# Seven small moves ahead of the first attention slot: first exponential, maxima, clearings, and who subtracts

## The chip, the cores and the metric

The kernel runs on one core of one Trainium2 chip. The metric is device time in microseconds (us); lower is better. A core has a matrix engine (TensorE, PE in the profile, its weight loads PEld), VectorE (DVE), ScalarE (ACT), GpSimd (POOL) and SyncE (SP), which here issues every DMA. Each engine works through its own instructions in order and waits at semaphores for the others. SBUF is the memory that all engines read and write; TensorE's results land in eight banks of PSUM.

## What is computed

`x` is 2048 x 512. With `xn` the row-normalised `x`, the output is attention times a gate, added to `x`:

```python
def _A_ref(x, wqkv, wo):                       # H = 32 heads of Dh = 16, window W = 256
    qkv = (x @ wqkv).reshape(B, S, 3, H, Dh).transpose(2, 0, 3, 1, 4)
    scores = jnp.einsum("bhqd,bhkd->bhqk", q, k) * (Dh ** -0.5)
    mask = (idx[:, None] - idx[None, :] >= 0) & (idx[:, None] - idx[None, :] < W)
    p = softmax(jnp.where(mask, scores, -1e9))
    return einsum(p, v).reshape(B, S, D) @ wo

def _B_ref(x, w1, b1, w2, b2):                 # F = 1792
    y = _layernorm(x)
    return _gelu(y @ w1 + b1) @ w2 + b2

return x + _A_ref(xn, ...) * _silu(_B_ref(xn, ...))
```

## The kernel before

**High and low parts.** Every matmul operand is split into a rounded high part and the rest, the low part, and a product is made of three passes (high x high, high x low, low x high; `PASSES`, line 67). The high part is a cast on ScalarE, the low part a subtraction on VectorE or GpSimd.

**Slots.** Attention is written as slots `t` = -16 to 128 (loop at line 896), one block of 128 queries of a group of four heads per slot: `prob_block` makes transposed scores in the PSUM tile `stb`, exponentiates them on ScalarE into `pt` and masks them on GpSimd (`affine_select`); it is called twice a slot, for head pair 1 and then for pair 0. `pv_step` multiplies with the values `vt` one slot later. `max_block(m)`, with m = t + 12, makes the plain scores in `xy` and `zo`, and VectorE masks them (`copy_predicated`) and reduces them to row maxima `mt`. `max_rows` sends the maxima of four blocks through DRAM (`mT_d`) into a row of the tile `slots[i]` (called qk0 and qk1), which holds the queries and keys of a head group.

**Projections fill the slots.** What TensorE does beside this in a slot is cut into two halves, `fill_in(t, 0)` and `fill_in(t, 1)`; `fills` says which matmuls stand in which half, `plan` what other work stands in a slot, `ends` (through `behind`) what ends it. Everything is emitted in that order, which is the order of every engine's queue, SP's too. `later(k, f)` puts f off by k halves. Slots -16 to -1 have no `prob_block`; in slots -8 to -1 the maxima block stands between the two halves.

**Jobs by halves.** `job_qk(n, c)` projects queries and keys of head group n for 512 tokens, `job_v(0, i)` the values of 256 tokens. From slot -8 on, `by_halves` runs such a job in two phases of 12 units; a unit is two matmuls side by side on the upper and lower 64 rows of the array, each into a bank of its own, and the second phase exchanges the banks. Before the second phase starts, the first must be through. That is seen to by a wait on a marker: for jobs with `by_max` it is the masked copy of the last maxima block, for the others a small memset of a column of the tile `sv` on GpSimd, which itself waits for the last unit. Jobs alternate between the banks `fb` (two tiles) and two banks of the pool `ps_st` (`others`, named pair_-8_599 and so on in the trace). At slot 0 that pool is closed, and `stb` takes its place.

**After a job.** For values, ScalarE copies the banks to `vt`. For queries and keys of group 1 (n = 1), ScalarE copies the banks to `pjr` (`raw`), casts it to `sh` (`hi`), and GpSimd subtracts. For group 0, ScalarE casts straight from the two banks and VectorE subtracts straight from them (lines 323 to 336). SP then issues four DMAs of the high part and two of the low part into `slots`.

**Other work.** `clear_part(k)` writes zeros or ones to a quarter of `slots[1]` on ScalarE, in slots -4 to -1 (lines 898 to 901). Slot 1's place in SBUF is that of the tile `x23`, which holds x for chunks 2 and 3; `job_x(3)` in slot -6 transposes the last of it, through `fb` and `ps_st`, into `xnT`. `split_wqk` makes the high part `wqb` of the weights of group 1 in slot -5 and the low part at the end of slot -4.

Of the kernel before, what the change touches and what calls it, by code (L numbers as in the profile page):

```python
# [9 lines left out]
F32 = mybir.dt.float32  # L10
# [5 lines left out]
PSUM = bass.MemoryType.PSUM  # L16

S, D, H, DH, WIN, F = 2048, 512, 32, 16, 256, 1792
P = 128
# [31 lines left out]
def mixer_kernel(ctx, tc, x, wqk, wv, wo, w1, b1, w2, b2, out):  # L51
# [132 lines left out]
    stb = []  # L184
# [96 lines left out]
    def later(k, fn):  # L281

        if k == 0:
            fn()
        else:
            h = 2 * now[0] + now[1] + k
            delayed.setdefault((h // 2, h % 2), []).append(fn)

    def job_qk(n, c):

        box = []
        ops = [(kt, a, b) for kt in range(KT) for a, b in PASSES]
        if not n and c < 3:
            ops.sort(key=lambda o: o[2])
        sl = slice(512 * c, 512 * (c + 1))

        def mm(i):
            if i == 0:
                box.append(fill_bank() if c else xy[:, 0])
            kt, a, b = ops[i]  # L300
            nc.tensor.matmul(box[0], wqs[n][:, a, kt], big[:, b, kt, sl],
                             start=(i == 0), stop=(i == len(ops) - 1))

        def half(bank, j, i, r, **flags):
            kt, a, b = ops[i]
            return nc.tensor.matmul(bank[:, 0:256], wqs[n][r, a, kt],
                                    big[r, b, kt, 512 * c + 256 * j: 512 * c + 256 * (j + 1)], **flags)

        def send(src, qk, tt):
            copy_rows(slots[n % 2][tt:P:4, qk, :, sl], src[64 * qk: 64 * qk + 64])  # L310

        def finish():
            hi = sgp.tile([P, 512], F32R, tag="sh", name=f"sh_{n}_{c}", bufs=2)
            raw = t2.tile([P, 512], F32, tag="t2", name=f"pjr_{n}_{c}")
            lo = raw.bitcast(F32R)
            if n:
                for j, bank in enumerate(box):
                    nc.scalar.copy(raw[:, 256 * j: 256 * (j + 1)], bank[:, 0:256])
                box[:] = [raw]
            wide = 512 // len(box)  # L320
            parts = [(bank[:, 0:wide], slice(wide * j, wide * (j + 1))) for j, bank in enumerate(box)]

            def high():
                for src, at_ in parts:
                    nc.scalar.copy(hi[:, at_], src)
                behind(now[0], send_high)

            def send_high():
                for qk, tt in ((1, 0), (0, 0), (1, 2), (0, 1)):
                    send(hi, qk, tt)  # L330

            def low():
                for src, at_ in parts:
                    (nc.gpsimd if n else nc.vector).tensor_tensor(lo[:, at_], src, hi[:, at_].bitcast(F32),
                                                                  op=ALU.subtract)
                behind(now[0], send_low)

            def send_low():
                send(lo, 1, 1)
                send(lo, 0, 2)  # L340

            later(1 if n else 0, high)
            later(3 if n else int(c < 3), low)
        if n or c > 1:
            return half, finish, box
        return [(216, mm, i) for i in range(len(ops))], finish

    def by_halves(job, banks, first, second, by_max=False):

        half, finish, box = job  # L350
        box[:] = banks
        seen = []
        for phase, where in enumerate((first, second)):
            for i in range(12):
                flags = dict(start=(phase == 0 and i == 0), stop=(phase == 1 and i == 11), skip_group_check=True)

                def unit(i=i, phase=phase, flags=flags):
                    if phase == 0 and i == 0:
                        box[:] = [bank() if callable(bank) else bank for bank in box]
                    two = (half(box[1 - phase], 1 - phase, i, slice(64, P), **flags),  # L360
                           half(box[phase], phase, i, slice(0, 64), **flags))
                    if phase == 0 and i == 11 and not by_max:
                        seen.append(nc.gpsimd.memset(sv[:, 31:32], 0.0))
                        for r in two:
                            tc.add_manual_dep(seen[0].ins, r.ins.name, ORDER, reason="the rows are through")
                    if phase == 1 and i == 0:
                        for r in two:
                            tc.add_manual_dep(r.ins, (seen or outs["max"])[0].ins.name, ORDER, reason="the banks change rows")
                fills.setdefault(where[len(where) * i // 12], []).append((unit, ()))
        fills[second[-1]].append((finish, ()))  # L370

    def job_v(hf, i):

        box = []

        def mm(k):
            if k == 0:
                box.append(ps_st.tile([P, 2, 256], F32, tag="b", name=f"pv_{hf}_{i}"))
            j, kt, (a, b) = k // 12, k % 12 // 3, PASSES[k % 3]
            kb = 2 * i + j  # L380
            nc.tensor.matmul(box[0][:, j], big[:, a, kt, P * kb: P * (kb + 1)], wva[:, b, kt],
                             start=(k % 12 == 0), stop=(k % 12 == 11))

        def half(bank, j, k, r, **flags):
            kt, (a, b) = k // 3, PASSES[k % 3]
            kb = 2 * i + j
            return nc.tensor.matmul(bank[:, 0:256], big[r, a, kt, P * kb: P * (kb + 1)], wva[r, b, kt], **flags)

        def finish():
            if i < 4:  # L390
                nc.scalar.copy(vt[:, 2 * i: 2 * i + 2, :, 0:DH], box[0].rearrange("p b (h d) -> p b h d", d=DH))
                return
            for j, bank in enumerate(box):
                nc.scalar.copy(vt[:, 2 * i + j, :, 0:DH], bank[:, 0:256].rearrange("p (h d) -> p h d", d=DH))
        if i > 3:
            return half, finish, box
        return [(109, mm, k) for k in range(24)], finish
# [336 lines left out]
    def at(t, fn, *args):  # L734
        plan.setdefault(t, []).append((fn, args))
# [61 lines left out]
        return ps_st.tile([P, 512], F32, tag="b", name=f"pair_{now[0]}")  # L797

    others = [free_bank, free_bank]
    for job, banks, first, second, *by_max in (  # L800
            (job_qk(0, 2), fb, [(-8, 0)], [(-7, 0)], True), (job_v(0, 4), others, [(-8, 0), (-8, 1)], [(-7, 1)]),
            (job_v(0, 5), fb, [(-5, 0)], [(-4, 0)], True), (job_qk(0, 3), others, [(-5, 1)], [(-4, 1)]),
            (job_v(0, 6), fb, [(-3, 0)], [(-2, 0)], True), (job_qk(1, 0), others, [(-3, 1)], [(-2, 1)]),
            (job_v(0, 7), fb, [(-1, 0)], [(-1, 1)]), (job_qk(1, 1), fb, [(0, 1), (1, 0)], [(2, 0), (2, 1)])):
        by_halves(job, banks, first, second, *by_max)
    fills.update(spread([job_x(3)], [(-6, 0), (-6, 1)]))
    fills[-10, 0][:0] = fills[-11, 1][-5:]
    del fills[-11, 1][-5:]
# [80 lines left out]
    def fill_in(t, half):  # L889
        now[:] = t, half  # L890
        run(delayed.pop((t, half), ()))
        for fn, args in fills.get((t, half), ()):
            fn(*args)

    end = 16 * NQ
    for t in range(-16, end + 1):
        m = t + LEAD
        if t == -5:
            open_slot(1)
            for k in range(4):  # L900
                at(-4 + k, clear_part, k)
        if 0 <= t < end:
            if t == 0:
                early.close()
                stb.append(attn.enter_context(tc.tile_pool(name="ps_s2", bufs=1, space=PSUM)).tile(
                    [P, 2, 512], F32, name="stb"))
            prob_block(t // 16, t % 16, 1)
        if t >= 0 and m < end:
            max_block(m // 16, m % 16, m not in IN_PLACE)
        fill_in(t, 0)  # L910
        for fn, args in plan.get(t, []):
            fn(*args)
        if 4 <= m < LEAD:
            max_block(0, m)
        if 0 <= t < end:
            prob_block(t // 16, t % 16, 0)
        fill_in(t, 1)
        if 0 <= m < 4:
            max_block(0, m)
        if t >= 0 and m + 1 < end and (m + 1) % 16 >= 2 and m + 1 not in IN_PLACE:  # L920
            first_scores((m + 1) // 16, (m + 1) % 16)
        if t >= 1:
            pv_step((t - 1) // 16, (t - 1) % 16)
        run(lns.get(t, ()))
        if 0 <= m < end and m % 4 == 3:
            max_rows(m // 16, m % 16 // 4, t)
        for fn, args in ends.get(t, []):
            fn(*args)
# [481 lines left out]
```

## Time and profile before

| | us |
|---|---|
| median of 3 runs | 737.11 (736.62 to 737.22) |
| the profiled execution | 736.99 |
| its span | 735.2 |
| TensorE busy | 720.2 |
| VectorE, ScalarE, GpSimd busy | 499.1, 426.0, 317.4 |

The attention slots that the change touches lie between 36 and 67 us of the span; slots 0 to 127 go on to about 424 us, and the MLP follows. TensorE's granted clock is full in all of the 40 slices. In a timeline row the columns are the start in us, the time until the last of the merged instructions ended, the engine, the operation, output<-inputs, the shape, the count, and in brackets the idle time in front with the engine that ended it. All instructions have the line 43, that of the helper which records them, so they are told apart by their tiles. A matmul's time is its way through the pipeline: starts, not durations, give the pace. In a row of stretches, the first number behind the stretch is its length, then come the busy times of PE, PEld, DVE, ACT and POOL with their instruction counts, the granted clock, the DMA engines' share and GB/s.

### The profile page before, as it was taken

Reading aid. Unit: us, or ns where it says so; the run is one execution under the profiler, and the core shown is the slowest. Engines: PE = TensorE matmul, PEld = TensorE weight load, DVE = VectorE, ACT = ScalarE, POOL = GpSimd, SP = SyncE. Lnnn points to the kernel's source line nnn. Section 1 sums busy time; section 2 is a strip of 40 time slices with the busy share of each in tenths; the row PEclk is TensorE's granted clock in tenths of the full one; section 3 lists DMA queues with packets and bytes.
Section 4 is the critical chain, followed back from the end, with each engine's and each line's share of the span. In section 5 each row is a group of like instructions: output and inputs, shape, how many; then the busy total and the mean of one; then the engine's idle time right before and its main releaser. Section 6 shows DMA issues by size and latency. Waiting matters only on the chain.

```text
span 735.2 us, 19063 instructions
## 1 busy us (share of the span) xinstructions
PE 720.2 (98%) x7584; PEld 586.3 (80%) x7584; DVE 499.1 (68%) x738; ACT 426.0 (58%) x721; POOL 317.4 (43%) x674
## 2 busy tenths in 40 slices
PE   8999999999999999999999999999999999999997
PEld 7988777777778887777776788888887888888886
DVE  6876767877766777777872666546687855666823
ACT  7747777868777676887877736232343734542001
POOL 7413667867677665777877640113202000001102
PEclk9999999999999999999999999999999999999999
DMA  8324256777766733667614376447223322153701
GB/s 296 78 47 105 66 146 162 216 233 213 209 187 189 205 121 103 164 170 199 194 63 160 105 256 165 180 130 242 87 57 101 115 73 86 60 185 115 247 23 58
DMA packets 61528, 106.77 MB, mean 145 GB/s; under 512 B 12096, under 2 KB 12352, under 8 KB 61440
## 3 DMA queue, kind: packets, MB, share of 16 engines
q1 hardware_dynamic: 61440, 105.56, 49.1%
q8 instruction: 60, 0.98, 0.5%
q14 instruction: 28, 0.23, 0.1%
HBM read 54.53 MB, written 33.82 MB: 120 GB/s over the span
## 4 chain that ended last, share of the span: by engine, by line
PE 90%; ACT 5%; DVE 2%; issue 1%; POOL 1%; DMA 1%; DVEq 0%; ACTq 0%; POOLq 0%
PE acc L43 20%; PE fb L43 19%; PE zo L43 13%; PE stb L43 9%; PE p L43 9%; PE s L43 6%; PE h L43 6%; PE xy L43 5%; ACT pt L43 3%; PE pv L43 1%; ACT x L43 1%; DVE xnT L43 1%; DVE xy L43 0%; ACT xnT L43 0%; DMA x<-in_x_dram 0%
## 5 line engine op out<-in xcount | busy, mean ns | idle before, releaser
L43 POOL TENSOR_SCALAR_AFFINE_SELECT pt<-pt 128x256 f32<-128x256 f32 x480 | 193.7, 428 | 99.6 <-ACT pt L43 94.4
L43 ACT ACTIVATE pt<-stb 128x768 f32<-128x768 f32 (+1 forms) x244 | 188.8, 774 | 45.4 <-PE stb L43 39.0
L43 DVE TENSOR_REDUCE mt<-xy 128x4 f32<-128x1024 f32 (+1 forms) x128 | 152.6, 1192 | 4.4
L43 DVE COPY_PREDICATED xy<-upper,zo 128x512 f32<-128x512 int32 x112 | 77.9, 695 | 73.8 <-PE xy L43 65.4
L43 POOL TENSOR_TENSOR xo<-xo,gated 128x512 f32<-128x512 f32 x15 | 20.0, 1331 | 220.9 <-DVE gated L43 219.9
L43 PE MATMUL zo<-pt,vt 128*17 128x128 f32 x2880 | 103.7, 275 | 0.0
L43 PE MATMUL stb<-qk 64*128 64x384 f32 (+1 forms) x488 | 94.9, 383 | 5.7 <-ACT pt L43 4.3
L43 PE MATMUL fb<-xnT,wqb 64*128 64x512 f32 (+2 forms) x732 | 99.6, 381 | 0.0
L43 PE MATMUL acc<-w,gh 128*128 128x512 f32 x320 | 98.6, 389 | 0.0
L43 PEld LDWEIGHTS stb<-qk 64*128 64x128 f32 x488 | 45.7, 183 | 49.2 <-ACT pt L43 40.3
L43 PEld LDWEIGHTS zo<-pt,vt 128*17 128x17 f32 x2880 | 67.5, 97 | 15.3 <-issue 4.9
L43 PEld LDWEIGHTS acc<-w,gh 128*128 128x128 f32 x320 | 60.1, 188 | 12.5
L43 PEld LDWEIGHTS fb<-xnT,wqb 64*128 64x128 f32 (+1 forms) x732 | 62.8, 185 | 6.5 <-DVE xy L43 0.2
L43 PE MATMUL acc<-w,gl 128*128 128x512 f32 x160 | 62.4, 390 | 0.2 <-DVE gl L43 0.2
L43 PE MATMUL xy<-qk 64*128 64x256 f32 (+2 forms) x536 | 58.4, 290 | 0.7 <-DVE mt L43 0.7
L43 PE MATMUL p<-xnT 128*128 128x512 f32 x189 | 51.8, 389 | 0.0
L43 PEld LDWEIGHTS xy<-qk 64*128 64x128 f32 x536 | 46.7, 185 | 6.1 <-issue 2.4
L43 ACT COPY oraw<-zo 128x128 f32<-128x128 f32 x108 | 28.8, 266 | 36.9 <-PE zo L43 30.1
L43 ACT ACTIVATE gated<-acc 128x512 f32<-128x512 f32 x16 | 8.7, 596 | 62.4 <-DVE acc L43 62.4
L43 PE MATMUL s<-wos,ohl 128*128 128x512 f32 (+1 forms) x204 | 44.3, 377 | 0.0
L43 PEld LDWEIGHTS s<-wos,ohl 128*128 128x128 f32 x204 | 36.8, 188 | 7.1
L43 PEld LDWEIGHTS p<-xnT 128*128 128x128 f32 x189 | 35.5, 188 | 7.4
(198 smaller groups left out, 1190.8 us busy)
## 6 DMA issues: line engine op xcount, KB each, us to landing
qk<-sh SPq DMA_DIRECT2D x128, 128.0 KB
qk<-pjr SPq DMA_DIRECT2D x64, 128.0 KB
oT_d<-oraw SPq DMA_DIRECT2D x32, 256.0 KB
w_d<-in_w_dram SPq DMA_DIRECT2D x14, 512.0 KB
xt_d<-xnT SPq DMA_DIRECT2D x12, 512.0 KB
x<-in_x_dram SPq DMA_DIRECT2D x16, 256.0 KB
w<-w_d SPq DMA_DIRECT2D x16, 256.0 KB
or<-oT_d SPq DMA_DIRECT2D x16, 256.0 KB
```

Of the source, the lines that this page charges most:

```text
L43: r = issue(*args, **kwargs)
```

## The change

- `job_qk(0, 3)` orders its units like the other chunks of group 0: those with the high part of xnT first.
- `job_qk(0, 2)` and `job_qk(0, 3)` now end as those of group 1 do: ScalarE copies the banks to `raw` and casts from there, GpSimd subtracts. The low part of chunk 3 comes one half later.
- The marker is named with each job: for `job_v(0, 4)` a memset on VectorE, for the other jobs that had a memset still one on GpSimd.
- `job_v(0, 7)`: its first phase spreads over both halves of slot -1, so that maxima block 11 stands after 6 units instead of 12, and its second phase is a third part of the slot.
- Between these two parts of slot -1 the pool is closed, `stb` is opened and the first `prob_block` of slot 0 (pair 1: scores, exponential, masks) is emitted, which stood at the head of slot 0.
- The four clearings stand in slots -5, -5, -4 and -3 instead of -4, -3, -2 and -1.

```diff
         ops = [(kt, a, b) for kt in range(KT) for a, b in PASSES]
-        if not n and c < 3:
+        if not n:
             ops.sort(key=lambda o: o[2])
...
-            if n:
+            if n or c > 1:
                 for j, bank in enumerate(box):
                     nc.scalar.copy(raw[:, 256 * j: 256 * (j + 1)], bank[:, 0:256])
                 box[:] = [raw]
...
-                    (nc.gpsimd if n else nc.vector).tensor_tensor(lo[:, at_], src, hi[:, at_].bitcast(F32),
+                    (nc.gpsimd if n or c > 1 else nc.vector).tensor_tensor(lo[:, at_], src, hi[:, at_].bitcast(F32),
                                                                   op=ALU.subtract)
...
-            later(3 if n else int(c < 3), low)
+            later(3 if n else 1, low)
...
-    def by_halves(job, banks, first, second, by_max=False):
+    def by_halves(job, banks, first, second, seer=None):
...
-                    if phase == 0 and i == 11 and not by_max:
-                        seen.append(nc.gpsimd.memset(sv[:, 31:32], 0.0))
+                    if phase == 0 and i == 11 and seer:
+                        seen.append(seer[0].memset(seer[1], 0.0))
...
-            (job_qk(0, 2), fb, [(-8, 0)], [(-7, 0)], True), (job_v(0, 4), others, [(-8, 0), (-8, 1)], [(-7, 1)]),
-            (job_v(0, 5), fb, [(-5, 0)], [(-4, 0)], True), (job_qk(0, 3), others, [(-5, 1)], [(-4, 1)]),
-            (job_v(0, 6), fb, [(-3, 0)], [(-2, 0)], True), (job_qk(1, 0), others, [(-3, 1)], [(-2, 1)]),
-            (job_v(0, 7), fb, [(-1, 0)], [(-1, 1)]), (job_qk(1, 1), fb, [(0, 1), (1, 0)], [(2, 0), (2, 1)])):
+    by_pool, by_dve = (nc.gpsimd, sv[:, 31:32]), (nc.vector, sv[:, 30:31])
+            (job_qk(0, 2), fb, [(-8, 0)], [(-7, 0)]), (job_v(0, 4), others, [(-8, 0), (-8, 1)], [(-7, 1)], by_dve),
+            (job_v(0, 5), fb, [(-5, 0)], [(-4, 0)]), (job_qk(0, 3), others, [(-5, 1)], [(-4, 1)], by_pool),
+            (job_v(0, 6), fb, [(-3, 0)], [(-2, 0)]), (job_qk(1, 0), others, [(-3, 1)], [(-2, 1)], by_pool),
+            (job_v(0, 7), fb, [(-1, 0), (-1, 1)], [(-1, 2)], by_pool),
+            (job_qk(1, 1), fb, [(0, 1), (1, 0)], [(2, 0), (2, 1)], by_pool)):
...
             for k in range(4):
-                at(-4 + k, clear_part, k)
-        if 0 <= t < end:
-            if t == 0:
-                early.close()
-                stb.append(...)
+                at(max(-5, k - 6), clear_part, k)
+        if 0 < t < end:
             prob_block(t // 16, t % 16, 1)
...
         fill_in(t, 1)
+        if t == -1:
+            early.close()
+            stb.append(...)
+            prob_block(0, 0, 1)
+            fill_in(t, 2)
```

More of the change, by code (lines that the diff above doesn't have):

```diff
@@ L799, in mixer_kernel @@
     others = [free_bank, free_bank]
-    for job, banks, first, second, *by_max in (
-            (job_qk(0, 2), fb, [(-8, 0)], [(-7, 0)], True), (job_v(0, 4), others, [(-8, 0), (-8, 1)], [(-7, 1)]),
-            (job_v(0, 5), fb, [(-5, 0)], [(-4, 0)], True), (job_qk(0, 3), others, [(-5, 1)], [(-4, 1)]),
-            (job_v(0, 6), fb, [(-3, 0)], [(-2, 0)], True), (job_qk(1, 0), others, [(-3, 1)], [(-2, 1)]),
-            (job_v(0, 7), fb, [(-1, 0)], [(-1, 1)]), (job_qk(1, 1), fb, [(0, 1), (1, 0)], [(2, 0), (2, 1)])):
-        by_halves(job, banks, first, second, *by_max)
+    by_pool, by_dve = (nc.gpsimd, sv[:, 31:32]), (nc.vector, sv[:, 30:31])
+    for job, banks, first, second, *seer in (
+            (job_qk(0, 2), fb, [(-8, 0)], [(-7, 0)]), (job_v(0, 4), others, [(-8, 0), (-8, 1)], [(-7, 1)], by_dve),
[3 more added lines that the diff above has]
+            (job_qk(1, 1), fb, [(0, 1), (1, 0)], [(2, 0), (2, 1)], by_pool)):
+        by_halves(job, banks, first, second, *seer)
     fills.update(spread([job_x(3)], [(-6, 0), (-6, 1)]))
@@ L900, in mixer_kernel @@
             for k in range(4):
-                at(-4 + k, clear_part, k)
-        if 0 <= t < end:
-            if t == 0:
-                early.close()
-                stb.append(attn.enter_context(tc.tile_pool(name="ps_s2", bufs=1, space=PSUM)).tile(
-                    [P, 2, 512], F32, name="stb"))
+                at(max(-5, k - 6), clear_part, k)
+        if 0 < t < end:
             prob_block(t // 16, t % 16, 1)
@@ L917, in mixer_kernel @@
         fill_in(t, 1)
+        if t == -1:
+            early.close()
+            stb.append(attn.enter_context(tc.tile_pool(name="ps_s2", bufs=1, space=PSUM)).tile(
+                [P, 2, 512], F32, name="stb"))
+            prob_block(0, 0, 1)
+            fill_in(t, 2)
         if 0 <= m < 4:
```

## The prediction

> **What bounds the kernel now.** I read the page first, then the busy times by stretch, then the waits and the timeline around every edit.
>
> ```profile
> span 735.2 us, 19063 instructions
> PE 720.2 (98%) x7584; PEld 586.3 (80%) x7584; DVE 499.1 (68%) x738; ACT 426.0 (58%) x721; POOL 317.4 (43%) x674
> ...
> 40.00:42.00 2.00, 0.94 (x16) 0.81 (x14) 1.79 (x2) 0.40 (x2) 1.14 (x3) 1.00 0.24 52
> 42.00:64.00 22.00, 21.57 (x322) 20.23 (x318) 16.04 (x25) 13.34 (x20) 0.30 (x3) 1.00 0.33 72
> 64.00:72.00 8.00, 7.14 (x96) 5.83 (x94) 6.43 (x10) 5.48 (x10) 5.05 (x12) 1.00 0.57 135
> 72.00:424.00 352.00, 346.35 (x5490) 271.53 (x5489) 248.06 (x315) 267.84 (x456) 247.86 (x580) 1.00 0.59 163
> ```
>
> TensorE is busy for 720.2 of 735.2 us, so an edit of the schedule can win only its idle time. The stretch rows (length, then TensorE's busy time) say where that lies: 1.06 us are lost between 40 and 42, 0.43 between 42 and 64, 0.86 between 64 and 72. All edits lie in slots -8 to 0, about 36 to 67 us. The stretch up to 424 us loses 5.65 us in small waits, each counted from work shortly before it and none from a fixed time, so I take a lead that stands at 72 us to last to the end. The profiled execution took 736.99 us, its span 735.2 with 1.8 around it; the median of the runs is 737.11. I work out the gain in the profiled execution and subtract it from the median, 0.12 above.
>
> **The change part by part.** *1. The memset of job_v(0,4) goes from GpSimd to VectorE.*
>
> ```profile
> 38.00 1.23 DVE L43 TENSOR_REDUCE mt<-xy 128x4 f32<-128x1024 f32 x1
> 38.02 1.70 PE L43 MATMUL fb<-xnT,wqb 64*128 64x256 f32 x24
> 39.55 0.40 PE L43 MATMUL xy<-qk 64*128 64x256 f32 x4
> 39.57 1.53 POOL L43 TENSOR_SCALAR x<-x,nm,rss 128x512 f32<-128x512 f32 x2
> 39.75 0.65 ACT L43 CAST sh<-fb 128x256 fp32r<-128x256 f32 x2 [1.10 <-PE fb L43]
> 41.04 0.10 POOL L43 MEMSET sv<- 128x1 f32 x1
> 41.19 0.38 PE L43 MATMUL pair_-8_599<-wva,xnT 64*128 64x256 f32 x1 [1.06 <-POOL sv L43]
> 42.05 0.74 DVE L43 TENSOR_TENSOR pjr<-fb,sh 128x256 fp32r<-128x256 f32 x2
> 42.82 1.09 PE L43 MATMUL fb<-ident,x 128*128 128x128 f32 x8
> ...
> 60.39 1.60 PE L43 MATMUL fb<-wva,xnT 64*128 64x256 f32 x24
> 61.83 0.40 PE L43 MATMUL xy<-qk 64*128 64x256 f32 x4
> 62.27 1.69 PE L43 MATMUL fb<-wva,xnT 64*128 64x256 f32 x24
> 62.45 0.70 DVE L43 COPY_PREDICATED xy<-upper,zo 128x512 f32<-128x512 int32 x1 [1.38 <-PE zo L43]
> 63.18 1.23 DVE L43 TENSOR_REDUCE mt<-xy 128x4 f32<-128x1024 f32 x1
> ```
>
> The second phase starts at 41.19 because the memset stands in GpSimd's queue behind two normalisations of x (39.57 to 41.10). A maxima block's matmuls take 0.44 us up to the next work (61.83 to 62.27); counted from 39.55 the phase could start at 39.99. On VectorE the memset stands behind a reduction ending at 39.23. Its cost there isn't in the trace: 0.10 as on GpSimd, or at most the 0.70 of a masked copy. Either ends by 39.93, in time; I take 0.10. Nobody waits behind it: the next masked copy waits for TensorE. Gain 1.20.
>
> What is late next? The transposes of x (42.82), which follow the phase, move to 41.62. Their x is ready at 41.10. They write fb, which VectorE's subtraction of job_qk(0,2) reads until 42.79: alone, the memset's move would win almost nothing. *2. That subtraction goes to GpSimd*, from a copy in SBUF, so fb is free after ScalarE's copies (40.40), and the whole 1.20 stands. It costs ScalarE one more 512-wide cast (0.63, from the 46.10 row below; ends near 41.0, and its next work is due at 41.7) and GpSimd 1.28 (the 66.20 row), behind the x tiles: 41.10 to 42.4, where VectorE ended at 42.79. SP's four high sends start 0.6 later, and the low ones behind them; the maxima block that reads them stands at 51.39, so even 1.20 sooner they have some 5 us.
>
> *3. Job_qk(0,3) likewise, and the clearings sooner.*
>
> ```profile
> 44.45 1.09 PE L43 MATMUL tr<-ident,x 128*128 128x128 f32 x8
> 46.10 0.63 ACT L43 CAST wqb<-wqkr 128x512 fp32r<-128x512 f32 x1
> 51.39 0.52 PE L43 MATMUL xy<-qk 64*128 64x256 f32 x4
> 51.59 0.65 ACT L43 COPY vt<-fb 128x256 f32<-128x256 f32 x2 [4.86 <-PE fb L43]
> 52.12 1.92 ACT L43 ACTIVATE qk<-vt 128x2048 fp32r<-128x2048 f32 x1
> 52.85 1.23 DVE L43 TENSOR_REDUCE mt<-xy 128x4 f32<-128x1024 f32 x1
> 53.29 1.72 PE L43 MATMUL fb<-wva,xnT 64*128 64x256 f32 x24
> 55.01 0.68 DVE L43 TENSOR_TENSOR wqb<-wqkr,wqb 128x512 fp32r<-128x512 f32 x1
> 55.43 0.28 PE L43 MATMUL pair_-3_927<-xnT,wqb 64*128 64x256 f32 x1
> 55.75 0.38 PE L43 MATMUL pair_-3_928<-xnT,wqb 64*128 64x256 f32 x1
> 57.16 1.18 SPq L43 DMA_DIRECT2D qk<-pjr  x2
> 58.69 0.65 ACT L43 COPY vt<-fb 128x256 f32<-128x256 f32 x2 [2.29 <-PE fb L43]
> 66.20 1.28 POOL L43 TENSOR_TENSOR pjr<-pjr,sh 128x512 fp32r<-128x512 f32 x1
> ```
>
> Units of a pair follow each other by 0.12 us (60.39 to 61.83 for twelve). The third unit of job_qk(1,0) should stand at 55.55 and stands at 55.75: it waits for the low part of wqb, which VectorE makes behind two subtractions of job_qk(0,3). With these gone it follows the reduction that ends at 54.08, so 52.9 to 53.6 with the lead of 1.20, against a need at 54.35. Gain 0.20.
>
> ScalarE's work is hidden by idle time. Clearings 0 and 1 follow the cast of wqb: 46.10 less 1.20 plus 0.63 is 45.53, plus 2 x 1.92 is 49.4; the next copies are due at 51.59 - 1.20 = 50.39, and ScalarE idles 4.86 before them now. Clearing 2 follows these copies to 52.9; then the copies out of job_qk(0,3)'s banks (0.65, to 53.6), whose next writer, job_qk(1,0), comes at 55.43 less two units and the lead, 54.0: 0.4 to spare. Cast (to 54.2) and clearing 3 (to 56.1) end ahead of the copies at 58.69 - 1.40 = 57.3. GpSimd's subtraction runs 54.2 to 55.5; its sends now stand in SP's queue behind a return of row maxima, so I put their issue at 58 to 59.2 instead of 57.16 to 58.34. They are read at 62.8 (below). Sorting the units changes their order, not their number: nothing.
>
> [...]
>
> *4. The boundary of slots -1 and 0.*
>
> ```profile
> 59.84 1.23 DVE L43 TENSOR_REDUCE mt<-xy 128x4 f32<-128x1024 f32 x1
> 62.12 0.10 POOL L43 MEMSET sv<- 128x1 f32 x1 [4.68 <-PE fb L43]
> 64.46 0.51 PE L43 MATMUL xy<-qk 64*128 64x256 f32 x4 [0.32 <-DVE mt L43]
> 65.44 0.44 PE L43 MATMUL stb<-qk 64*128 64x384 f32 x2 [0.30 <-ACT pt L43]
> 65.72 0.87 PE L43 MATMUL fb<-xnT,wqb 64*128 64x256 f32 x12
> 65.91 1.23 DVE L43 TENSOR_REDUCE mt<-xy 128x4 f32<-128x1024 f32 x1
> 67.19 0.50 PE L43 MATMUL xy<-qk 64*128 64x256 f32 x4
> ```
>
> I count from job_v(0,7)'s first unit (60.39 before). Now: fb of job_qk(1,1) at +5.33, the maxima block of slot 1 at +6.80. After: six units, 0.72; maxima block 11 (the reduction it waits for ends at 61.07, +0.68, just in time), 0.44; six units, the last issued at +1.76; first scores, 0.28 (65.44 to 65.72), to +2.16. The second phase waits for GpSimd's memset: before, it started 0.56 after the last unit's issue (61.71 to 62.27), so +2.32, a wait of 0.16. Twelve units to +3.76; block 12, 0.44; second scores, 0.28; so fb at +4.48. ScalarE must have copied fb: with ScalarE free, copies began 0.41 after a job's last unit (38.02 + 11 x 0.12 = 39.34, to 39.75) and took 0.65, so +3.64 + 1.06 = +4.70. TensorE would gain 0.63. VectorE: block 12's masked copy 0.62 after its matmuls (61.83 to 62.45), reduction 0.73 later, 1.23 long: +6.34, so slot 1's block at +6.39; TensorE itself would be there at +4.70 + 1.47 = +6.17. VectorE comes last: gain 0.41, bounds 0.41 and 0.63. Both waits named in the rows go; the exponential no longer ends them.
>
> Sum: 1.20 + 0.20 + 0.41 = 1.81, by the upper bound 2.03. 737.11 - 1.81 = 735.3, 0.25% less.
>
> **The rivals.** *VectorE's loop takes part 4.* Masked copy and reduction, 2 us with the matmuls between, already end only 0.04 ahead of block 11. If they or the memset cost 0.4 more, only 1.40 is left: 735.7. For it: part 4 already ends on VectorE; against: the extra must last past slot 2.
>
> *Part 1 moves its wait.* If the transposes still wait, for x, fb or ScalarE, 0.3 of the 1.20 is won: with the rest 0.9, 736.2. For it: three things must be ready at 41.6. Against: the latest is x, 0.5 ahead. [...]
>
> *Slower: the clearings stand in front.* Slot 1's place holds x until the transposes (44.45 plus 1.09, less 1.20: 44.3). Were it free late, clearings 0 and 1 would hold up ScalarE's copies of job_v(0,5), which free fb for the matmuls at 53.29. The copies have 1.0 to spare and fb another 1.0 (53.29 - 1.20 against 50.39 + 0.65), so every us of start beyond 47.6 costs TensorE one; beyond 49.4 the gain is gone. If the first started where it does now (52.12 - 1.20 = 50.9), 3.3 is lost: 738.6. Against: no row has a reader of x after the transposes.
>
> *The change does not do what it says*, the scores being held by the pool that they are moved into: then part 4 alone falls, the first rival's 735.7.
>
> **How the numbers follow.** About 0.2% (1.47 us, 735.64) is what a measurement of this kernel can tell from no change. Forecast 0.70 (735.3, own range 734.8 to 735.7, of which 0.06 lies above 735.64); part 4 lost, for either cause, 0.15 (735.7, a third of it below 735.64); moved wait or lock 0.10 (736.2 to 736.4); slower 0.05 (738.6). Faster: 0.64 + 0.05 = 0.69; same 0.25; slower 0.06 with unnamed mishaps. The range reaches down to 734.6 for small waits of 64 to 72 us that may go beyond the 2.03, and up to 736.6 for the moved wait; what it leaves out is the slower case and edges.
>
> **What would show it.** Right: no TensorE wait for sv near 40; transposes of x near 41.6; TensorE idle between 40 and 42 near 0.1; four clearings ended by 56.5; the first exponential near 61, ahead of job_v(0,7)'s copies; slot 1's maxima block near 65.4, not 67.19; the same lead at 424. Wrong: a wait for fb, x or wqb in its place, ScalarE clearing past 50, or a lead that shrinks later.

## The result, and the profile after

The changed kernel takes 735.17 us (median of 18 runs, 734.74 to 736.18) against 736.88 for the kernel before (18 runs beside them); the ratio is 0.9978, 95% interval 0.9972 to 0.9985, or 1.7 us less. The forecast was 735.3 within 734.6 to 736.6.

The page's head of the changed kernel and its stretches, columns as before:

```profile
span 734.4 us, 19062 instructions
PE 721.2 (98%) x7584; PEld 588.1 (80%) x7584; DVE 498.6 (68%) x735; ACT 427.7 (58%) x723; POOL 319.5 (44%) x675
...
40.00:42.00 2.00, 2.00 (x38) 2.00 (x36) 1.02 (x4) 1.27 (x3) 1.96 (x4) 1.00 0.04 8
42.00:64.00 22.00, 21.50 (x322) 20.18 (x322) 16.78 (x24) 15.19 (x23) 3.93 (x8) 1.00 0.38 84
64.00:72.00 8.00, 7.32 (x110) 5.86 (x108) 5.77 (x6) 5.37 (x11) 4.84 (x12) 1.00 0.48 113
72.00:424.00 352.00, 346.20 (x5473) 271.72 (x5472) 247.67 (x314) 267.82 (x454) 246.93 (x579) 1.00 0.59 164
```

The hole between 40 and 42 is gone. The span of this execution (736.18 us in all, the slowest of the 18) is only 0.8 below that of the one before, because it began late: maxima block 5, ahead of every edit, stands at 40.40 instead of 39.55. So I compare the traces from block 5's matmuls on. To slot 1's maxima block it is 27.64 us before and 25.87 after, 1.77 less; from there to the end of the span 668.0 and 668.1. The lead is whole at slot 1 and stays whole.

The timeline around the first place, and of slots -5 to 1:

```profile
40.02 0.06 DVE L43 MEMSET sv<- 128x1 f32 x1
40.40 0.40 PE L43 MATMUL xy<-qk 64*128 64x256 f32 x4
40.60 0.65 ACT L43 COPY pjr<-fb 128x256 f32<-128x256 f32 x2 [1.10 <-PE fb L43]
40.82 0.33 PE L43 MATMUL pair_-8_599<-wva,xnT 64*128 64x256 f32 x1
41.98 1.28 POOL L43 TENSOR_TENSOR pjr<-pjr,sh 128x512 fp32r<-128x512 f32 x1
42.39 1.09 PE L43 MATMUL fb<-ident,x 128*128 128x128 f32 x8
46.19 3.72 ACT L43 ACTIVATE qk<-vt 128x2048 fp32r<-128x2048 f32 x2
53.56 0.68 DVE L43 TENSOR_TENSOR wqb<-wqkr,wqb 128x512 fp32r<-128x512 f32 x1
54.71 1.90 ACT L43 ACTIVATE qk<-vt 128x2048 fp32r<-128x2048 f32 x1
55.00 0.28 PE L43 MATMUL pair_-3_928<-xnT,wqb 64*128 64x256 f32 x1
59.10 1.23 DVE L43 TENSOR_REDUCE mt<-xy 128x4 f32<-128x1024 f32 x1
59.54 0.99 PE L43 MATMUL fb<-wva,xnT 64*128 64x256 f32 x12
60.38 0.51 PE L43 MATMUL xy<-qk 64*128 64x256 f32 x4
60.89 0.93 PE L43 MATMUL fb<-wva,xnT 64*128 64x256 f32 x12
61.66 0.34 PE L43 MATMUL stb<-qk 64*128 64x384 f32 x2
61.95 0.10 POOL L43 MEMSET sv<- 128x1 f32 x1 [5.26 <-PE fb L43]
62.04 0.81 ACT L43 ACTIVATE pt<-stb 128x768 f32<-128x768 f32 x1 [0.96 <-PE stb L43]
62.10 1.69 PE L43 MATMUL fb<-wva,xnT 64*128 64x256 f32 x24
63.63 0.40 PE L43 MATMUL xy<-qk 64*128 64x256 f32 x4
64.26 0.70 DVE L43 COPY_PREDICATED xy<-upper,zo 128x512 f32<-128x512 int32 x1 [0.28 <-PE zo L43]
64.53 0.98 PE L43 MATMUL fb<-xnT,wqb 64*128 64x256 f32 x12
66.27 0.51 PE L43 MATMUL xy<-qk 64*128 64x256 f32 x4 [0.36 <-DVE mt L43]
```

The marker ends at 40.08, the second phase follows block 5 after 0.42, the transposes stand 1.99 after it (3.27 before). The clearings end by 56.6. The first exponential starts at 62.04, ahead of job_v(0,7)'s copies. Both waits of part 4, for VectorE at 64.46 and for ScalarE at 65.44 in the profile before, are gone; what TensorE now waits for is VectorE, 0.36 at slot 1's block. With the 0.85 by which this execution began late taken off, the transposes, the end of the clearings, the first exponential and slot 1's block stand at 41.54, 55.8, 61.2 and 65.42, where the prediction named 41.6, 56.5, 61 and 65.4.

### The profile page after: what moved, and what is told of

The parts are those of the page before. It is cut to its first block, busy times and chain, and to the rows that moved or that the text cites. A ratio compares the mean times of both kernels' runs of the same rounds, so it can differ in the third digit from the quotient of the medians.

```text
span 734.4 us, 19062 instructions
## 1 busy us (share of the span) xinstructions
PE 721.2 (98%) x7584; PEld 588.1 (80%) x7584; DVE 498.6 (68%) x735; ACT 427.7 (58%) x723; POOL 319.5 (44%) x675
## 4 chain that ended last, share of the span: by engine, by line
PE 92%; ACT 3%; DVE 2%; issue 1%; DMA 1%; POOL 0%; DVEq 0%; ACTq 0%; POOLq 0%
PE fb L43 20%; PE acc L43 20%; PE zo L43 14%; PE p L43 9%; PE stb L43 9%; PE s L43 6%; PE h L43 6%; PE xy L43 5%; ACT pt L43 2%; PE pv L43 2%; DVE xy L43 1%; DVE xnT L43 1%; DVE mt L43 1%; DMA x<-in_x_dram 0%; PE tr L43 0%
```

## The experiments

Each kernel ran against the kernel before on one chip; its ratio is worked out over all the runs and need not be the quotient of the two medians. Below, "interval" is the time from block 5's matmuls to slot 1's maxima block in the profiled execution (27.64 before, 25.87 changed).

**The marker alone** (the kernel before with `job_v(0, 4)` marked by `by_dve`):

```diff
-seen.append(nc.gpsimd.memset(sv[:, 31:32], 0.0))
+seen.append(seer[0].memset(seer[1], 0.0))        # VectorE for job_v(0, 4), GpSimd else
```

> The kernel before with one edit: the marker of job_v(0,4) is a memset on VectorE; subtractions, clearings and the boundary stay. My theory: the second phase starts 1.20 us sooner after maxima block 5, but the transposes of x write fb, which VectorE reads for job_qk(0,2) until 2.5 us after that block's reduction began, so they stay where they are: nothing gained, 0.0 to -0.1 us against the kernel before. Rival (each edit wins by itself): -1.2 us. From block 5's matmuls to slot 1's block: 27.6 us by the theory, 26.4 by the rival.

Measured: 736.93 against 736.75, ratio 1.0003 (0.9994 to 1.0012); interval 27.39.

```profile
39.52 0.40 PE L43 MATMUL xy<-qk 64*128 64x256 f32 x4
39.94 0.33 PE L43 MATMUL pair_-8_599<-wva,xnT 64*128 64x256 f32 x1
42.58 0.63 PE L43 MATMUL fb<-ident,x 128*128 128x128 f32 x4 [0.99 <-DVE pjr L43]
```

The phase starts at 39.94, and a wait of 0.99 us comes back in front of the transposes, now put down to VectorE's subtraction from fb. The interval is still 0.25 shorter than before, which my theory did not have: the transposes start at 42.58, between the ends of VectorE's two subtractions (42.43 and 42.76 in this trace). So they need only the first of the two, and stand 3.06 after block 5 instead of 3.27.

**The low parts alone:**

```diff
-            if n:
+            if n or c > 1:
...
-                    (nc.gpsimd if n else nc.vector).tensor_tensor(...)
+                    (nc.gpsimd if n or c > 1 else nc.vector).tensor_tensor(...)
```

> The kernel before with the low parts of job_qk(0,2) and (0,3) on GpSimd from a copy in SBUF (and the units sorted); marker, clearings and boundary stay. My theory: only the wait for wqb's low part goes, -0.2 us; the wait for the marker near 40 stays at 1.06. From block 5's matmuls to slot 1's block: 27.4. Rival (the added ScalarE casts and the GpSimd subtractions cost something): 0.0 to +0.6 us.

(The delay and the order of the units go with it.) Measured: 736.41 against 736.75, ratio 0.9998 (0.9989 to 1.0007); interval 27.28. The waits of this kernel on TensorE have the marker's again:

```profile
PE pair_-8_599 L43 <- POOL sv L43: 1.0, 1, 1.0
```

**Both together:**

> Both: marker on VectorE and low parts on GpSimd; clearings and boundary stay. My theory: the two need each other, -1.40 us (more than the sum of each alone, -0.2 to -0.3); from block 5's matmuls to slot 1's block 26.2. Rival (additive): the sum of the two single kernels.

Measured: 735.36 against 736.75, ratio 0.9981 (0.9972 to 0.9990), 1.39 less; interval 26.05, 1.59 less, where the two alone win 0.25 and 0.36. They need each other: the transposes stand 3.06 after block 5 with the marker alone, 3.21 with the low parts alone and 1.99 with both, so each edit removes one of two waits that end within 0.2 us of each other.

**The boundary alone** (block 11 after 6 units, first scores ahead of the second phase; clearings as before):

> The kernel before with the boundary of slots -1 and 0 alone (maxima block 11 after 6 units, first scores and exponential ahead of the second phase); the clearings stay in slots -4 to -1. My theory: the first exponential stands on ScalarE behind the cast and the last clearing, which ends at 64.15, so it starts there and not at 61.8; job_v(0,7)'s copies follow it and free fb at 65.7, as late as now: 0.0 us (-0.1 to +0.1), and TensorE waits for ScalarE at fb or stb near 65. Rival (the clearings don't matter): -0.4 us.

Measured: 736.66 against 736.75, ratio 1.0001 (0.9992 to 1.0009); interval 27.40. The time shows nothing; the trace shows 0.24, between theory and rival.

**All but the boundary:**

> The changed kernel with the boundary as before: marker on VectorE, low parts on GpSimd, clearings in slots -5 to -3. My theory: the clearings alone win nothing, since the first exponential waits for the first scores, which still follow the second phase: -1.4 us against the kernel before, the same as without moving the clearings. Rival (the sooner clearings let the first exponential go): -1.8 us.

Measured: 735.49 against 736.82, ratio 0.9981 (0.9972 to 0.9990), 1.33 less; interval 26.03, the same as with the clearings where they were (26.05). Moving the clearings wins nothing here.

**The clearings late:**

```diff
-                at(max(-5, k - 6), clear_part, k)
+                at(-4 + k, clear_part, k)
```

> The changed kernel with the clearings where they were, in slots -4 to -1. My theory: the last clearing holds the first exponential and, behind it, job_v(0,7)'s copies, which free fb; part 4 turns into a loss of some 0.3 us: -1.1 us against the kernel before, 0.7 worse than the changed kernel, with a TensorE wait for ScalarE at stb or fb near 64. Rival (ScalarE has room enough): -1.8 us.

Measured: 735.17 against 736.82, ratio 0.9977 (0.9967 to 0.9987), 1.65 less; interval 25.86. The theory fell. ScalarE and TensorE of this kernel:

```profile
60.33 1.91 ACT L43 ACTIVATE qk<-vt 128x2048 fp32r<-128x2048 f32 x1
62.15 0.79 ACT L43 ACTIVATE pt<-stb 128x768 f32<-128x768 f32 x1
62.83 0.64 ACT L43 COPY vt<-fb 128x256 f32<-128x256 f32 x2
62.98 0.44 PE L43 MATMUL stb<-qk 64*128 64x384 f32 x2
```

The last clearing does hold the exponential, to 62.15, but that ends at 62.94, just as TensorE comes to the next scores at 62.98. I had added full durations along ScalarE, while in the rows each instruction starts about 0.1 before the one ahead of it ends (the clearing ends at 62.24, the exponential starts at 62.15). From the copies at 56.74 in this trace to the end of that clearing 5.50 us pass, while the durations add up to 5.87, so such a sum ends 0.37 late.

**Chunk 3 on VectorE:**

```diff
-            if n or c > 1:
+            if n or c == 2:                          # subtraction and delay likewise, units unsorted
```

> The changed kernel with job_qk(0,3) as before: VectorE subtracts from the two banks, units unsorted, low part at once. My theory: the wait for wqb's low part comes back, 0.2 us worse than the changed kernel: -1.6 us against the kernel before; in the trace a gap of 0.2 at the third unit of job_qk(1,0). Rival (VectorE's time there is free): -1.8 us.

Measured: 735.73 against 736.82, ratio 0.9984 (0.9975 to 0.9993), 1.09 less; interval 26.52, 0.65 worse than the changed kernel, and job_v(0,7) starts 19.55 after block 5 instead of 19.14. VectorE makes wqb's low part at 53.33 to 54.01, behind the two subtractions, and job_qk(1,0)'s third unit follows at 54.07, 0.44 behind the unit before instead of 0.11. So 0.41 is the wait for wqb's low part, and the rest goes with a late marker:

```profile
54.07 0.38 PE L43 MATMUL pair_-3_930<-xnT,wqb 64*128 64x256 f32 x1
...
61.37 0.10 POOL L43 MEMSET sv<- 128x1 f32 x1 [5.61 <-PE stb L43]
61.52 1.69 PE L43 MATMUL fb<-wva,xnT 64*128 64x256 f32 x24 [0.46 <-POOL sv L43]
```

By the trace the last matmul of the first phase was issued at 60.60, and the memset came 0.77 later, against 0.41 in the changed kernel (61.54 to 61.95), with GpSimd idle for 5.6 us; the next expectation took the last unit 0.05 too early and says 0.81 and 0.46. Block 11 gives 0.1 of it back: it stands 0.74 after the job's first unit instead of 0.84.

**The same program again:**

> The kernel with job_qk(0,3) as before, a second look at the same program. In its first trace the marker of job_v(0,7) came 0.35 us later after the last unit than in the changed kernel (0.81 against 0.46), with nothing in GpSimd's queue. If that belongs to the program, it is there again, and slot 1's block comes 26.5 us after block 5; if it was chance, the marker comes at 0.46 and the block at 26.1.

Measured (a single run): 735.67; the marker again 0.77 after the last matmul (61.04 to 61.81), interval 26.55. It belongs to the program.

**Chunk 3 on VectorE, from SBUF and a half later:**

```diff
-(nc.gpsimd if n or c > 1 else nc.vector).tensor_tensor(lo[:, at_], ...)
+(nc.gpsimd if n or c == 2 else nc.vector).tensor_tensor(lo[:, at_], ...)
```

> The changed kernel with the subtraction of job_qk(0,3) on VectorE, but from the copy in SBUF and a half later, as in the changed kernel. My theory: what counts is that wqb's low part comes ahead of it and that the banks are free, not the engine: as fast as the changed kernel (-1.7 us against the kernel before, 25.9 us from block 5 to slot 1's block). Rival (only an empty VectorE helps): 0.5 us worse, because maxima block 9's masked copy comes 0.6 us later.

Measured: 735.55 against 736.77, ratio 0.9983 (0.9974 to 0.9991), 1.22 less; interval 26.22, 0.35 worse. Job_v(0,7) starts 19.23 after block 5, within 0.1 of the changed kernel: for wqb, order counts and not the engine. What is lost is the late marker once more:

```profile
61.59 0.10 POOL L43 MEMSET sv<- 128x1 f32 x1 [5.61 <-PE stb L43]
```

**Units unsorted:**

> The changed kernel with the units of job_qk(0,3) in the old order. My theory: nothing changes, since the job's first unit waits for its banks until the last low part of xnT is through anyway: 25.9 us from block 5 to slot 1's block, the same gap of 0.2 before the second matmul. Rival (the sorting hides a wait for low parts): 0.2 us more.

Measured (a single run): 735.39; interval 25.86 and the marker at 0.41. In this trace the sorting does nothing.

**Four clearings in slot -4:**

```diff
-                at(max(-5, k - 6), clear_part, k)
+                at(-4, clear_part, k)
```

> The changed kernel with all four clearings in slot -4: the slower rival's mechanism, made on purpose. My theory: ScalarE works through them in order from 51.7 to 59.3 of the span; the copies out of job_qk(0,3)'s banks follow at 59.9, and job_qk(1,0), due at 54.7, waits 5.2 us: 5 us worse than the changed kernel, 740.2. Rival (slack downstream takes most of it): under 2 us worse.

Measured: 742.07 against 736.82, ratio 1.0070 (1.0056 to 1.0084), 6.9 worse than the changed kernel; interval 33.24. The wait, and stretches with the granted clock (the number ahead of the last two):

```profile
58.52 0.58 PE L43 MATMUL pair_-3_928<-xnT,wqb 64*128 64x256 f32 x1 [4.33 <-ACT pjr L43]
61.31 2.97 PE L43 MATMUL fb<-wva,xnT 64*128 64x256 f32 x24
...
57.50:58.00 0.50, 0.00 (x0) 0.00 (x0) 0.00 (x0) 0.50 (x1) 0.00 (x0) 0.83 0.00 0
58.00:58.50 0.50, 0.00 (x0) 0.00 (x0) 0.00 (x0) 0.50 (x3) 0.00 (x0) 0.50 0.00 0
64.00:64.50 0.50, 0.50 (x9) 0.50 (x6) 0.00 (x0) 0.38 (x2) 0.00 (x0) 0.50 0.85 209
65.00:66.00 1.00, 1.00 (x21) 1.00 (x20) 0.97 (x2) 0.00 (x0) 0.00 (x0) 1.00 0.05 12
```

The mechanism is the one expected, its price is higher. TensorE idles 4.33 us, not 5.2; near the end of that its granted clock falls to 0.50 and stays there until about 64.7, so 24 matmuls take 2.97 us instead of 1.7. Some 6 us at half speed cost about 3 more (7.37 in the interval less 4.33).

**Block 11 after 8 units:**

```diff
-            (job_v(0, 7), fb, [(-1, 0), (-1, 1)], [(-1, 2)], by_pool),
+            (job_v(0, 7), fb, [(-1, 0), (-1, 0), (-1, 1)], [(-1, 2)], by_pool),
```

> The changed kernel with one edit: maxima block 11 stands after 8 units of job_v(0,7) instead of 6. In the changed kernel's trace that block waits 0.1 us for the reduction before it, and its reduction is the last thing only after block 12's matmuls, so block 11 may stand later without holding VectorE. My theory: block 12 comes 3.8 to 3.9 us after the job's first unit instead of 4.1, slot 1's block 6.4 to 6.5 instead of 6.73: 0.2 to 0.3 us less than the changed kernel in the trace (from block 5's matmuls to slot 1's block 25.6 instead of 25.87), too little for the time to show. Rival (VectorE is the bound from block 10 on, whatever the place of block 11): no change or later.

Measured: 735.91 against 736.77, ratio 0.9991 (0.9982 to 1.0000), only 0.86 less; interval 26.62, 0.75 worse than the changed kernel. My theory fell; later is what the rival allowed, but what held VectorE is not in it. GpSimd, VectorE and TensorE of this kernel:

```profile
62.57 1.28 POOL L43 TENSOR_TENSOR pjr<-pjr,sh 128x512 fp32r<-128x512 f32 x1
62.66 1.22 DVE L43 TENSOR_TENSOR mh<-mt,mh 128x16 fp32r<-128x16 f32 x1
64.05 0.67 DVE L43 COPY_PREDICATED xy<-upper,zo 128x512 f32<-128x512 int32 x1
66.03 0.51 PE L43 MATMUL xy<-qk 64*128 64x256 f32 x4 [0.60 <-DVE mt L43]
```

Block 12's matmuls came 0.1 sooner after the job's first unit (3.98 against 4.09), but VectorE's small subtraction on `mh`, the tile with the parts of the row maxima, now fell beside GpSimd's subtraction of job_qk(1,0). It took 1.22 us instead of 0.18 and ended with it (63.88 and 63.85), and block 12's masked copy waited behind.

## Why the prediction was right, point by point

**Place and total.** Interval 1.77 less against a sum of 1.81, time 1.7 less. That the sum is so close is partly luck: part 1 came out 0.08 and part 3 0.22 better than forecast, part 4 0.34 worse.

**Part 1.** 1.20 was predicted, the transposes show 1.28 (3.27 to 1.99). That the marker alone would win almost nothing, and that the subtraction's move is what makes the gain stand, is shown by the three kernels; in the kernel with chunk 3 on VectorE, where only job_qk(0,2)'s subtraction has moved, maxima block 6 still stands 3.01 after block 5, as in the changed kernel (4.29 before). That fb is read until 42.79 was taken too late for the first transposes: they need only the first half of the subtraction.

**Part 3** was predicted at 0.20 and brought 0.42: job_v(0,6)'s second phase stood 17.50 after block 5 and stands at 15.80. I took the natural place of job_qk(1,0)'s third unit from the second matmul of the unit before (55.43), while a unit follows the first one (55.31): 0.33 lost instead of 0.20, and some 0.1 more for the restart behind the wait (the next unit follows at 55.97, after 0.22, where those behind it stand 0.12 apart). The kernel with chunk 3 on VectorE gives 0.41 of it back. From the profile before:

```profile
55.31 0.28 PE L43 MATMUL pair_-3_928<-xnT,wqb 64*128 64x256 f32 x1
57.05 1.60 PE L43 MATMUL fb<-wva,xnT 64*128 64x256 f32 x24
58.91 0.33 PE L43 MATMUL pair_-3_927<-xnT,wqb 64*128 64x256 f32 x1
58.91 0.33 PE L43 MATMUL pair_-3_928<-xnT,wqb 64*128 64x256 f32 x1
```

and from the changed kernel:

```profile
58.06 0.33 PE L43 MATMUL pair_-3_927<-xnT,wqb 64*128 64x256 f32 x1
58.17 0.33 PE L43 MATMUL pair_-3_928<-xnT,wqb 64*128 64x256 f32 x1
```

The last rows show a side effect that the prediction did not have. Before, the two matmuls of a unit start together from the wait for wqb on (55.75, 58.91); in the changed kernel they stay 0.11 apart up to block 11. They start together in every kernel here that has this wait, and about 0.1 apart in those without it, but for the one in which VectorE subtracts chunk 3 from SBUF, where block 10 comes 0.09 late and they are 0.03 apart. That costs part 4 about 0.11.

**Part 4** was predicted at 0.41 and brought 0.07: from job_v(0,7)'s first unit to slot 1's block 6.80 before, 6.73 after, 6.39 forecast. The mechanism was right (VectorE last, both old waits gone), the links were short: block 11 waits 0.12 for the reduction (+0.84 for +0.72), which ends later because block 10's matmuls are 0.11 apart too; the last unit comes at +2.00 for +1.76; the second phase starts the forecast 0.56 after it, and its twelve units take 1.53 instead of 1.44 after the wait. From there on the forecast holds: masked copy 0.63 after block 12, reduction 0.73 later and 1.23 long. The boundary edit by itself is worth 0.18: from job_v(0,7)'s first unit to slot 1's block it takes 6.62 in the kernel with the boundary alone, where the matmuls of a unit start together, against 6.80 before, and 6.73 in the changed kernel, where they are 0.11 apart, against 6.91 in the kernel without the boundary. So the 1.77 are made up of 1.28 and 0.42, less 0.11, and 0.18. The time, with intervals of 0.1%, cannot separate the kernels with and without the boundary.

**The clearings** were put at nothing, and nothing they are: 25.86 late, 25.87 early. I had also thought them needed for part 4; they are not.

**The rivals.** Most of part 4 was lost, as the first rival had it, but not to masked copies, reductions or a memset that cost more: of the 0.34 only block 11's 0.12 is a wait for VectorE, the rest is TensorE's own way to block 12; part 3's surplus paid for it. The moved wait exists where only the marker is moved. Clearings that stand in front do make the kernel slower, at a higher price than I gave, but this is shown for job_qk(0,3)'s copies and not for job_v(0,5)'s, which the prediction named; in the changed kernel the first clearing starts at 46.19, right behind the cast of wqb. No run shows the lock that is counted with the moved wait, nor its 736.4: in the changed kernel wqb's low part kept clear of GpSimd (53.56 to 54.24, 0.68 long as in the profile before; GpSimd's subtraction from 54.88). What the runs show in its place is VectorE's subtraction on `mh` beside GpSimd's, 1.22 us instead of 0.18, in the kernel with block 11 after 8 units, and it held block 12's masked copy.

**Left open:** why the marker of job_v(0,7) comes 0.36 later in the kernels with chunk 3 on VectorE that are made from the changed one. The engine that subtracts is not enough of a cause: in the kernel before, with the marker alone and with the boundary alone VectorE subtracts too, and the marker comes at 0.41. Nor is it TensorE: though the profile puts the wait down to the first scores (stb), the instruction ahead of the memset, with which GpSimd waits for TensorE, stands 0.32 after the last matmul in all of these traces, and the memset 0.08 behind it in the changed kernel and 0.44 in the late ones. Counted in the traces, the late marker has 68 instructions of GpSimd ahead of it, those that come in time 67, 69 or 71; whether its place in the stream is the cause no run here tests.

## What to carry to other kernels

When one wait is removed, ask at once what the work behind it waits for: here the waits for the marker and for the buffer's reader ended within 0.2 us of each other, and in the trace the two edits alone won 0.25 and 0.36, together 1.59. Compare two profiled executions from an event ahead of the edits, since the start alone moved by about half the gain (39.55 and 40.40). A bound that ends only 0.04 us ahead in a sum is to be counted as a wait.

## What was not expected of the hardware

A tiny VectorE subtraction, that on `mh`, took 1.22 us instead of 0.18 beside a GpSimd subtraction of 1.28 (the kernel with block 11 after 8 units). In the changed kernel the same pair of `mh` instructions takes 0.28 and 0.33 instead of 0.17 and 0.18, beside the masking of the first exponential:

```profile
62.93 0.78 POOL L43 TENSOR_SCALAR_AFFINE_SELECT pt<-pt 128x256 f32<-128x256 f32 x2 [0.88 <-ACT pt L43]
63.09 0.28 DVE L43 CAST mh<-mt 128x16 fp32r<-128x16 f32 x1
63.41 0.33 DVE L43 TENSOR_TENSOR mh<-mt,mh 128x16 fp32r<-128x16 f32 x1
```

The two masking instructions merged in the first row end at 63.34 and 63.71 in the trace, and the cast and the subtraction 0.03 behind them, at 63.37 and 63.73. There it is hidden, since VectorE then idles 0.28 for TensorE. And within a TensorE wait of 4.33 us the granted clock fell from 1.00 to 0.50: by the stretches of the kernel with four clearings in slot -4 it fell 3.6 us after the last matmul (54.19 to 57.8) and came back 6.1 us after work resumed (58.52 to 64.7).
